# Chunks 10 and 11 of k and q through TensorE transposes, and a reordered load list, in a windowed-attention and SwiGLU kernel

## The chip, the core and the metric

The program runs on one core of one Trainium2 chip. The metric is the time of one execution on the device in microseconds (us): the median over several runs. Beside it there is one execution recorded by the hardware profiler, whose instructions, DMAs and idle times are the views quoted in this document.

## What is computed

Attention over 8 batches of 8 heads, with 576 positions of 64 elements each, where each position sees itself and the 63 before it. Its output, as 4608 tokens of 512 elements, goes through a gated feed-forward block.

```python
scores = scale * np.matmul(q, k.transpose(0, 1, 3, 2))
mask = (rel >= 0) & (rel < window)          # window = 64, rel = query - key
attn = softmax of scores where mask holds
x = np.matmul(attn, v), laid out as (4608, 512)
g = x @ w_gate                              # (512, 1536)
silu = g * (1.0 / (1.0 + np.exp(-g)))
val = x @ w_val                             # (512, 1536)
return (silu * val @ w_out)                 # (1536, 512)
```

q, k, v and the weights lie in HBM as float32; the kernel casts them to bf16 on the way in.

## The kernel before, in words

**Tiles.** The 4608 tokens are 36 chunks of 128. Attention works on a chunk at a time, mostly in pairs; the feed-forward block works on groups of 512 tokens (`c` = 0 to 8), so four chunks feed one group. For each chunk the scores (`S`, `Sb`, `S2`, `Sx`: L459 to L534) need k and q with the head dimension on the partitions (`kT`, `qT`), the product with v (`AV2`, `B2`: L602, L712) needs the probabilities `pt` and the values `va`, and its normalised result `xb` is transposed (`X`: four TensorE transposes at L804, or one DMA transpose at L791) into `xT`, which feeds the group.

**The feed-forward block.** `F(c, fs)` computes `hT` for the 128-row blocks `fs` of the 1536 hidden rows: four matmuls of 128x512 by `Wg`, four by `Wv` (L908), a tanh on ScalarE (L889), two operations on VectorE (L894, L896). `F(c, (a, b), lo, hi)` does two blocks on half of the tokens, with matmuls of 128x256. `O` and `O2` (L950) multiply `hT` by `Wo`, twelve matmuls for each 128 tokens, and store.

**Four ways to kT and qT.** (1) Chunks 0 to 3: loaded in a row layout (`first_loads`, `next_load`), transposed by `first_T`. (2) `load2` brings a pair of chunks into `ks2[st % 2]`, `qs2[st % 2]`, and `T64(st)` does 64 small TensorE transposes (L389: 2 tensors, 8 columns, 2 chunks, 2 halves), evicted in four copies by ScalarE; used for pairs 2 and 4, that is chunks 4, 5 and 8, 9. (3) `next_load(x, 3)` and `T64(3)` do the same for chunks 6 and 7 from the row layout. (4) All others: `load(n, "kq")` on GpSimd's queue and a DMA transpose on SyncE's queue (`T`, L368).

**Buffers that matter here.** Way 1 for chunks 2, 3 and way 3 use one pair of buffers, `ks1` and `qs1`; it is `self.first[x, 1]` (L216, L217), with the keys `("s2", x, 1, 0)` and `("s2", x, 1, 1)`. `load2` for pairs 2 and 4 uses `ks0` and `qs0`.

**What sets the order.** The order is written by hand in `build` (L1040). Each call of `g.op` appends one operation; `_Graph.op` (L43) notes as its dependencies the operations that last wrote what it reads, and those that last read or wrote what it writes, as the program stands at that call. Each engine runs its operations in the order in which they were appended, and waits at each for its dependencies. All loads but the first four DMAs are issued from GpSimd (POOL) in one queue. The program order around the change is this (L1106 to L1115):

```python
        self.Tkq2(2)
        self.late_loads()
        F(0, (7,))
        self.S2(4)
        F(0, (8,))
        F(0, (9,), side=True)
        self.AV2(4)
        F(0, (10,))
        ev = self.T64(3)
```

`early_loads` is called at L1065, while chunks 0 to 3 are worked on, `more_loads` at L1100. PSUM has eight banks, taken in the order of least recent use (`bank`, L230).

Of the kernel before, what the change touches and what calls it, by code (L numbers as in the profile page):

```python
# [152 lines left out]

class _Kernel:
    NQ = 8
    NV = 10
    NZ = 8
    ZQ = 9
# [14 lines left out]
    def alloc(self):  # L173
        nc = self.nc

        def sb(name, n, dtype=BF):
            return nc.alloc_sbuf_tensor(name, [128, n], dtype)

        def ring(name, cnt, n, dtype=BF):
            return [sb("%s%d" % (name, i), n, dtype) for i in range(cnt)]  # L180
# [8 lines left out]
        self.Wo = sb("Wo", NF * DM)[:, :].rearrange("p (c m) -> p c m", c=NF)  # L189
        self.qn = ring("qn", self.NQ, DM)  # L190
        self.kn = ring("kn", self.NQ, DM)
        pair = lambda t: t[:, :].rearrange("p (h j d) -> p h j d", h=H, j=2)
        qs, ks = ring("qs", 2, 2 * DM), ring("ks", 2, 2 * DM)
        self.qs2 = [pair(t) for t in qs]
        self.ks2 = [pair(t) for t in ks]
        self.va = [t[:, :].rearrange("p (h d) -> p h d", h=H) for t in ring("va", self.NV, H * 80)]
        self.vs = [t[:, :].rearrange("p (h d) -> p h d", h=H) for t in ring("vs", 3, H * 80)]
# [41 lines left out]
    def pair(self):  # L239
        if not self.lru:  # L240
            return [self.bank("a"), self.bank("a")]
        ok = [j for j in range(0, 8, 2) if not {j, j + 1} & self.held]
        j = min(ok, key=lambda j: max(self.touched(j), self.touched(j + 1)))
        self.held |= {j, j + 1}
        return [(self.ps[i], ("ps", i)) for i in (j, j + 1)]
# [68 lines left out]
    def load(self, n, what="kqv", gate=None):  # L314
# [3 lines left out]
        for x in what:  # L318
            src = {"k": self.k, "q": self.q, "v": self.v}[x]
            if x == "v":  # L320
                dst, nm, i = self.va[n % self.NV], "va", n % self.NV
            else:
                i = n % self.NQ
                dst = (self.kn if x == "k" else self.qn)[i][:, :].rearrange("p (h d) -> p h d", h=H)
# [35 lines left out]
    def T(self, n, x):  # L360
        if n >= NCH:
            return
        i = n % self.NQ
        if x == "k":
# [6 lines left out]
    def T64(self, st):  # L371
        n = 2 * st
        bx = self.two()
        loads = []
        for x in "kq":
            if st == 3:
                loads.append((x, *self.first[x, 1]))
            else:
                loads.append((x, (self.ks2 if x == "k" else self.qs2)[st % 2], [("s2", x, st % 2, i) for i in range(2)]))

        def pe(e):
            for i, (x, src, _) in enumerate(loads):
                for a in range(8):
                    for u in range(2):
                        r = slice(64 * u, 64 * u + 64)
                        for p in range(2):
                            o = bx[u][0].bitcast(BF)[64 * p:64 * p + 64, 512 * i + 64 * a:512 * i + 64 * a + 64]
                            y = src[r, a, p, :] if st == 3 else src[r, 2 * (a // 2) + p, a % 2, :]
                            z = e.transpose(o, y, self.ident[r, r])  # L389
            return z  # L390

        rd = ["ident"] + [k for _, _, ks in loads for k in ks]
        self.g.op("pe", pe, reads=rd, writes=[b[1] for b in bx])

        def ev(x, u, eng):
            bank, bk = bx[u]
            i = "kq".index(x)
            a = bank.bitcast(BF)[:, 512 * i:512 * i + 512]
            z = (n + u) % (self.NZ if x == "k" else self.ZQ)
            d = (self.kT if x == "k" else self.qT)[:, :, 128 * z:128 * z + 128]  # L400
            if st == 3:
                a, d = a.rearrange("p (j g c) -> p c g j", j=8, c=4), d.rearrange("p c (g j) -> p c g j", j=8)
            else:
                a, d = a.rearrange("p (c j t) -> p c t j", c=4, j=2), d.rearrange("p c (t j) -> p c t j", j=2)
            self.copy(eng, d, a, [bk], [(x + "T", z, 0), (x + "T", z, 1)])
            left.discard((x, u))
            if not any(v == u for _, v in left):
                self.held.discard(bk[1])

        left = {(x, u) for x in "kq" for u in range(2)}  # L410
        return ev
# [135 lines left out]
    def AVk(self, st, phase):  # L547
        n, bx, av, done = st
        iv, jv, ip, jp = n % self.NV, (n - 1) % self.NV, n % self.NP, (n - 1) % self.NP
        lone = [(2 * n) % BPB == 0, (2 * n + 1) % BPB == 0]  # L550
# [35 lines left out]
    def AVmm(self, st, phase):  # L586
        n, bx, av, done = st
        iv, jv, ip = n % self.NV, (n - 1) % self.NV, n % self.NP
        va, vb, pt = self.va[iv], self.va[jv], self.pt[ip]
# [82 lines left out]
    def unit(self, n, h, r, c):  # L672
        iv, jv, ip, jp = n % self.NV, (n - 1) % self.NV, n % self.NP, (n - 1) % self.NP
        rows = slice(64 * r, 64 * r + 64)
        back = r == 1 and c == 0
        va = self.va[jv if back else iv][rows, h, 0:65]
        if n < self.KW:
            return self.pt[ip][rows, h, 64 * c:64 * c + 64], va
        if c != r and (2 * n + c) % BPB == 0:
            return None  # L680
        x0 = 0 if c == r else 64
        return self.pt[jp if back else ip][rows, h, x0:x0 + 64], va

    def AVpair(self, n):
# [6 lines left out]
        def part(m, phase, js, after=None):  # L691
# [22 lines left out]

            iv, jv, ip, jp = m % self.NV, (m - 1) % self.NV, m % self.NP, (m - 1) % self.NP
            rd = [("pt", a, p) for a in ({ip, jp} if m >= self.KW else {ip}) for p in range(2)]
# [65 lines left out]
    def X(self, n, eng="sp", kind="f"):  # L782
        if n >= NCH:
            return
        g = self.g
        ix, it, u = n % 4, (n // 4) % self.NX, n % 4
        xb = self.xb[ix]
        xo = self.xT[it][:, :, 128 * u:128 * u + 128]
        xk = [("xb", ix, 0), ("xb", ix, 1)]
        if eng == "sp":  # L790
            g.op("sp", lambda e: e.dma_start_transpose(xo, xb[:, :]), reads=xk, writes=[("xT", it, u)], dma=True)  # L791
            return
        self.Xp(n, kind)(eng)
# [122 lines left out]
    def F(self, c, fs, lo=0, hi=512, mid=None, side=False):  # L916
        do = self.Fp(c, fs, lo, hi, side)
        for a in range(len(fs)):
            do("Wg", a)
        if mid:  # L920
            mid()
        do("tan", 0)
        for a in range(len(fs)):
            do("Wv", a)
        do("end", 0)
# [4 lines left out]
    def O(self, c, u, mid=None):  # L930
        io = (4 * c + u) % self.NO
        self.Omm(c, u, 0, 512, "act", [("ost", io), ("osth", io)], mid=mid)
        self.store(c, u)
# [70 lines left out]
    def early_loads(self):  # L1004
        self.load2(2, "k")
        self.load2(2, "q")
        self.W(8, 10)
        self.W(10, 12)
        self.load(4, "v")
        self.load(5, "v")  # L1010

    def more_loads(self):
        self.next_load("k", 3)
        self.next_load("q", 3)
        self.load_wo(0, 6)
        self.load_wo(6, 12)
        self.load(6, "v")
        self.load(7, "v")

    def late_loads(self):  # L1020
        for n in (10, 11):
            self.load(n, "kq")
        self.load2(4, "k")
        self.load2(4, "q")
        for n in (8, 9):
            self.load(n, "v")
        for n in (12, 13):
            self.load(n, "kq")

    def loop_loads(self, n):  # L1030
        for m in (n + 6, n + 7):
# [8 lines left out]
    def build(self):  # L1040
        F, S, AV, X, O = self.F, self.S, self.AV, self.X, self.O
# [68 lines left out]
        F(0, (8,))  # L1110
        F(0, (9,), side=True)
        self.AV2(4)
        F(0, (10,))
        ev = self.T64(3)
        ev("k", 0, "act")  # L1115
        ev("q", 0, "act")
        X(4, "act")
        F(0, (11,), mid=lambda: X(5, "act"))
        ev("k", 1, "act")
        ev("q", 1, "act")  # L1120
        F(1, (0, 1), 0, 256)
        self.S2(6)
        F(1, (2, 3), 0, 256)
        O(0, 0)
        self.AV2(6)
        for n in (10, 11):
            self.Tkq(n)

        def mid():
            X(6, "act")  # L1130
            X(7, "dve")

        O(0, 1, mid)
        F(1, (4,))
        self.init_kmask()
        F(1, (5,))
        self.Tkq2(4)
        for n in (10, 11):
            self.load(n, "v", self.lastF)
        for n in (12, 13):  # L1140
            self.Tkq(n)
        F(1, (6,))
        self.S2(8)
        F(1, (7,))
        self.O2(0, 2)
        self.B2(8)
        self.store(0, 2)
        X(8)
        X(9)
        F(1, (0, 1), 256, 512)  # L1150
        F(1, (8,))
        for n in (14, 15):
            self.load(n, "kq", self.lastF)
        F(1, (2, 3), 256, 512)
        self.O2(0, 3)
        self.B2(10)
        self.store(0, 3)
        F(1, (9,))
        self.T(14, "k")
        X(10)  # L1160
        X(11)
# [10 lines left out]
        for c in range(2, NFC):  # L1172
            for u in range(4):
                n = 4 * c + u + 4
# [6 lines left out]
                v = u + 1 if c == 2 else u  # L1181
# [71 lines left out]
```

## Time and profile before

| | us |
|---|---|
| runs | 329.48, 328.05, 329.32 |
| median | 329.32 |
| profiled execution | 327.78 |
| its span, first to last instruction | 325.9 |
| TensorE (PE) busy | 319.0 |
| VectorE (DVE) busy | 215.6 |
| ScalarE (ACT) busy | 125.8 |
| GpSimd (POOL) busy | 104.1 |

The profiled execution lasts 1.88 us longer than its span. PE is matmuls, PEld weight loads that overlap them, SP is SyncE; a q behind an engine's name (POOLq, SPq) marks a DMA that it issued. In a timeline row stand the start, the duration of the merged group, engine, line, operation, output<-inputs, shape and count, and in brackets the idle time of the engine just before and what ended it. In a row of DMA issues the last number is the time from issue to landing, when its semaphore tells that all data is there. L12 is line 12 of the kernel.

### The profile page before, as it was taken

What the parts mean: (1) busy time and instruction counts of PE and PEld (TensorE: products, weight loads), DVE (VectorE), ACT (ScalarE), POOL (GpSimd) and SP (SyncE); (2) the same over time, 40 slices, a digit from 0 to 9 for tenths busy, and PEclk for the clock granted to TensorE, in tenths of its full rate; (3) what the DMA queues carried; (4) which work ended last, traced back from release to release, by engine and by line L of the source; (5) the groups of instructions that cost most, each with busy time, mean ns of one, the idle gap of its engine ahead of it and who ended that gap; (6) DMA issues with size and microseconds to landing.
All of it is one profiled execution on the core that took longest, in us unless ns stands there. A gap on an engine that the chain in (4) does not pass through costs nothing.

```text
span 325.9 us, 7911 instructions
## 1 busy us (share of the span) xinstructions
PE 319.0 (98%) x3374; PEld 161.9 (50%) x3374; DVE 215.6 (66%) x400; ACT 125.8 (39%) x227; POOL 104.1 (32%) x134
## 2 busy tenths in 40 slices
PE   7999999899999999999999999999999999999996
PEld 5654564465444554545444454545454544444444
DVE  6776875588485967675858595858676767555510
ACT  3836554634232533333324242424242421322311
POOL 6999832041726052607060606151402000000000
PEclk9999999999999999999999999999999999999999
DMA  7999999999999979979999997999796404000012
GB/s 187 178 192 186 206 172 174 146 140 149 154 152 155 134 86 148 154 122 145 131 102 126 141 153 74 139 137 131 102 116 92 74 32 66 32 32 34 32 64 97
DMA packets 154354, 39.83 MB, mean 122 GB/s; under 512 B 140368, under 2 KB 149328, under 8 KB 154320
## 3 DMA queue, kind: packets, MB, share of 16 engines
q0 software_dynamic: 104896, 18.36, 72.4%
q1 hardware_dynamic: 43952, 11.15, 23.8%
q10 hardware_dynamic: 5472, 9.83, 9.8%
q8 instruction: 26, 0.43, 0.6%
q14 instruction: 8, 0.07, 0.1%
HBM read 37.75 MB, written 9.44 MB: 145 GB/s over the span
## 4 chain that ended last, share of the span: by engine, by line
PE 94%; DMA 2%; POOL 2%; DVE 1%; issue 1%
PE ps L908 58%; PE ps L950 29%; PE ps L712 2%; DMA Wv<-in_moe_w_val_dram 2%; PE ps L534 2%; PE ps L484 1%; POOL va L330 1%; PE ps L389 1%; PE ps L488 1%; PE ps L602 0%; PE ps L804 0%; POOL ks L828 0%; PE ps L565 0%; POOL qs L828 0%; POOL Wg L345 0%
## 5 line engine op out<-in xcount | busy, mean ns | idle before, releaser
L894 DVE SCALAR_TENSOR_TENSOR uu<-sig,ps 128x512 bf16<-128x512 bf16 x108 | 73.8, 683 | 57.6 <-ACT sig L889 57.2
L908 PE MATMUL ps<-xT,Wv 128*128 128x512 bf16 (+1 forms) x456 | 110.9, 368 | 0.5 <-DMA Wv<-in_moe_w_val_dram 0.5
L908 PE MATMUL ps<-xT,Wg 128*128 128x512 bf16 (+1 forms) x456 | 111.1, 368 | 0.0
L889 ACT ACTIVATE sig<-ps 128x512 bf16<-128x512 f32 x108 | 65.2, 604 | 90.3 <-PE ps L908 90.3
L950 PE MATMUL ps<-Wo,hT 128*128 128x512 bf16 (+1 forms) x444 | 98.8, 373 | 0.0
L896 DVE SCALAR_TENSOR_TENSOR hT<-uu,ps 128x512 bf16<-128x512 bf16 x108 | 74.2, 687 | 4.2 <-PE ps L908 0.5
L908 PEld LDWEIGHTS ps<-xT,Wv 128*128 128x128 bf16 x456 | 44.5, 98 | 49.1 <-DMA Wv<-in_moe_w_val_dram 0.6
L950 PEld LDWEIGHTS ps<-Wo,hT 128*128 128x128 bf16 x444 | 43.3, 98 | 49.2
L908 PEld LDWEIGHTS ps<-xT,Wg 128*128 128x128 bf16 x456 | 42.7, 98 | 45.3 <-ACT xT L260 0.4
L330 POOL DMA_DIRECT2D kn<-in_k_dram x29 | 24.9, 861 | 109.7 <-PE ps L908 105.4
L330 POOL DMA_DIRECT2D va<-in_v_dram x40 | 34.2, 885 | 33.5 <-PE ps L908 33.5
L260 ACT ACTIVATE ost<-ps 128x512 f32<-128x512 f32 (+1 forms) x22 | 12.9, 588 | 52.9 <-PE ps L950 52.9
L261 DVE COPY ost<-ps 128x512 f32<-128x512 f32 (+1 forms) x15 | 10.1, 674 | 30.9 <-PE ps L950 30.9
L544 ACT ACTIVATE pt<-ps 128x512 bf16<-128x512 f32 x36 | 18.6, 602 | 29.0 <-PE ps L534 29.0
L330 POOL DMA_DIRECT2D qn<-in_q_dram x29 | 25.1, 871 | 0.3 <-issue 0.3
L496 ACT ACTIVATE pt<-ps 128x512 bf16<-128x512 f32 x28 | 14.5, 615 | 13.2 <-PE ps L488 13.2
L747 DVE TENSOR_TENSOR xb<-ps,rc 128x512 bf16<-128x512 f32 (+2 forms) x39 | 18.8, 509 | 0.5
L712 PE MATMUL ps<-va,pt 64*64 64x65 bf16 x800 | 12.5, 192 | 0.8 <-issue 0.8
L510 DVE TENSOR_TENSOR pt<-pt,kmask 128x1024 bf16<-128x1024 bf16 x18 | 11.5, 681 | 0.0
L712 PEld LDWEIGHTS ps<-va,pt 64*64 64x64 bf16 x800 | 10.4, 107 | 0.9 <-issue 0.9
L743 DVE RECIPROCAL rc<-ps 128x8 f32<-128x8 f32 (+2 forms) x39 | 5.7, 173 | 7.6 <-PE ps L712 7.1
L510 DVE TENSOR_TENSOR pt<-pt,mask 128x1024 bf16<-128x1024 bf16 x14 | 9.2, 685 | 0.4 <-ACT pt L496 0.3
(76 smaller groups left out, 132.5 us busy)
## 6 DMA issues: line engine op xcount, KB each, us to landing
out_dram<-ost ACTq DMA_DIRECT2D x35, 256.0 KB, 3.1
va<-in_v_dram POOLq DMA_DIRECT2D x32, 128.0 KB, 5.3
kn<-in_k_dram POOLq DMA_DIRECT2D x23, 128.0 KB, 4.5
qn<-in_q_dram POOLq DMA_DIRECT2D x23, 128.0 KB, 4.5
Wg<-in_moe_w_gate_dram POOLq DMA_DIRECT2D x6, 256.0 KB, 6.6
Wv<-in_moe_w_val_dram POOLq DMA_DIRECT2D x6, 256.0 KB, 7.7
Wo<-in_moe_w_out_dram POOLq DMA_DIRECT2D x2, 768.0 KB, 17.0
ks<-in_k_dram POOLq DMA_DIRECT2D x2, 256.0 KB, 7.4
```

The source lines that it names most:

```text
L260: return self.g.op("act", lambda e: e.activation(d, a, ACTF.Copy), reads=reads, writes=writes, after=after)
L330: self.g.op("pool", lambda e, d=d, a=a: e.dma_start(d, a), writes=ks, dma=True, after=gate)
L496: g.op("act", lambda e, po=po, p=p: e.activation(po, sv[p], ACTF.Exp, scale=SCALE), reads=[bx[p][1]], writes=[pk[p]])
L510: self.g.op("dve", lambda e: e.tensor_tensor(pt, pt, m, ALU.mult), reads=pk + mk, writes=pk)
L544: g.op("act", lambda e, po=po, p=p: e.activation(po, sv[p], ACTF.Exp, scale=SCALE), reads=[bx[p][1]], writes=[pk[p]])
L712: x = e.matmul(o, ab[0], ab[1], start=first, stop=phase == 1, skip_group_check=True)
L747: g.op("dve", lambda e, av=av, hs=hs, w=w, rc=rc, xo=xo: e.tensor_tensor(xo[:, :, hs, :], av[:, :, :, 0:64], rc[:, :, hs].unsqueeze(3).to_ ...
L889: g.op("act", lambda e: e.activation(sig[:, 0:w], G[:, 0:w], ACTF.Tanh, scale=0.5), reads=[gk], writes=[("sig", i)])
L894: g.op("dve", lambda e: e.scalar_tensor_tensor(uu[:, 0:w], sig[:, 0:w], 1.0, G[:, 0:w], ALU.add, ALU.mult), reads=[("sig", i), gk], writes ...
L896: g.op("dve", lambda e: e.scalar_tensor_tensor(out, v3(uu), 0.5, v3(V), ALU.mult, ALU.mult), reads=[("uu", i), vk], writes=[("hT", ih, f) ...
L908: r = e.matmul(bank[:, a * n:a * n + n], W[:, kk, f * 128:f * 128 + 128], xT[:, kk, lo:hi], start=(kk == 0), stop=(kk == NK - 1))
L950: r = e.matmul(OB[:, 0:n], hT[:, f, 128 * u:128 * u + 128], self.Wo[:, f, lo:hi], start=(f == 0), stop=(f == NF - 1))
```

## The change

`ROWS = (3, 5)` lets `T64(5)` take chunks 10 and 11 in the row layout, as `T64(3)` does for 6 and 7. Their `load(n, "kq")` and their four DMA transposes go; `next_load("k", 5)` and `next_load("q", 5)` come, in `late_loads`, into the buffers of `self.first[x, 1]`. `next_load` for pair 3 moves into `early_loads`, ahead of `W(10, 12)`, as do the values of chunks 4 and 5. The values of chunks 10 and 11 are loaded at the end of `late_loads` and no longer wait for a matmul group. `T64(3)` moves from behind `F(0, (10,))` to directly behind `AV2(4)`, `Tkq2(4)` from behind `F(1, (5,))` to directly behind `AV2(6)`, and `Tkq2(5)` stands directly behind `S2(8)`. The blocks of group 1 are run in another order: blocks 4 and 5 in two halves, 6 and 7 whole but later, 8 and 9 earlier. The calls of L1106 to L1112 stay as they are.

```diff
--- before.py
+++ after.py
@@ -153,6 +153,7 @@
 
 class _Kernel:
     NQ = 8
+    ROWS = (3, 5)
     NV = 10
     NZ = 8
     ZQ = 9
@@ -373,7 +374,7 @@
         bx = self.two()
         loads = []
         for x in "kq":
-            if st == 3:
+            if st in self.ROWS:
                 loads.append((x, *self.first[x, 1]))
             else:
                 loads.append((x, (self.ks2 if x == "k" else self.qs2)[st % 2], [("s2", x, st % 2, i) for i in range(2)]))
@@ -385,7 +386,7 @@
                         r = slice(64 * u, 64 * u + 64)
                         for p in range(2):
                             o = bx[u][0].bitcast(BF)[64 * p:64 * p + 64, 512 * i + 64 * a:512 * i + 64 * a + 64]
-                            y = src[r, a, p, :] if st == 3 else src[r, 2 * (a // 2) + p, a % 2, :]
+                            y = src[r, a, p, :] if st in self.ROWS else src[r, 2 * (a // 2) + p, a % 2, :]
                             z = e.transpose(o, y, self.ident[r, r])
             return z
 
@@ -398,7 +399,7 @@
             a = bank.bitcast(BF)[:, 512 * i:512 * i + 512]
             z = (n + u) % (self.NZ if x == "k" else self.ZQ)
             d = (self.kT if x == "k" else self.qT)[:, :, 128 * z:128 * z + 128]
-            if st == 3:
+            if st in self.ROWS:
                 a, d = a.rearrange("p (j g c) -> p c g j", j=8, c=4), d.rearrange("p c (g j) -> p c g j", j=8)
             else:
                 a, d = a.rearrange("p (c j t) -> p c t j", c=4, j=2), d.rearrange("p c (t j) -> p c t j", j=2)
@@ -1005,27 +1006,29 @@
         self.load2(2, "k")
         self.load2(2, "q")
         self.W(8, 10)
-        self.W(10, 12)
         self.load(4, "v")
         self.load(5, "v")
-
-    def more_loads(self):
         self.next_load("k", 3)
         self.next_load("q", 3)
+        self.W(10, 12)
+
+    def more_loads(self):
         self.load_wo(0, 6)
         self.load_wo(6, 12)
         self.load(6, "v")
         self.load(7, "v")
 
     def late_loads(self):
-        for n in (10, 11):
-            self.load(n, "kq")
         self.load2(4, "k")
         self.load2(4, "q")
         for n in (8, 9):
             self.load(n, "v")
+        self.next_load("k", 5)
+        self.next_load("q", 5)
         for n in (12, 13):
             self.load(n, "kq")
+        for n in (10, 11):
+            self.load(n, "v")
 
     def loop_loads(self, n):
         for m in (n + 6, n + 7):
@@ -1110,52 +1113,49 @@
         F(0, (8,))
         F(0, (9,), side=True)
         self.AV2(4)
-        F(0, (10,))
         ev = self.T64(3)
         ev("k", 0, "act")
         ev("q", 0, "act")
+        ev("k", 1, "act")
+        ev("q", 1, "act")
+        F(0, (10,))
         X(4, "act")
         F(0, (11,), mid=lambda: X(5, "act"))
-        ev("k", 1, "act")
-        ev("q", 1, "act")
         F(1, (0, 1), 0, 256)
         self.S2(6)
         F(1, (2, 3), 0, 256)
         O(0, 0)
+        F(1, (4, 5), 0, 256)
         self.AV2(6)
-        for n in (10, 11):
-            self.Tkq(n)
+        self.Tkq2(4)
 
         def mid():
             X(6, "act")
             X(7, "dve")
 
         O(0, 1, mid)
-        F(1, (4,))
+        F(1, (8,))
         self.init_kmask()
-        F(1, (5,))
-        self.Tkq2(4)
-        for n in (10, 11):
-            self.load(n, "v", self.lastF)
+        self.S2(8)
+        self.Tkq2(5)
         for n in (12, 13):
             self.Tkq(n)
-        F(1, (6,))
-        self.S2(8)
-        F(1, (7,))
+        F(1, (9,))
+        F(1, (0, 1), 256, 512)
         self.O2(0, 2)
         self.B2(8)
         self.store(0, 2)
         X(8)
         X(9)
-        F(1, (0, 1), 256, 512)
-        F(1, (8,))
+        F(1, (2, 3), 256, 512)
+        F(1, (6,))
         for n in (14, 15):
             self.load(n, "kq", self.lastF)
-        F(1, (2, 3), 256, 512)
+        F(1, (4, 5), 256, 512)
         self.O2(0, 3)
         self.B2(10)
         self.store(0, 3)
-        F(1, (9,))
+        F(1, (7,))
         self.T(14, "k")
         X(10)
         X(11)
```

## The prediction

> **What bounds the kernel now.** I read the page's list of busy time first, then the chain that ended last.
>
> ```profile
> PE 319.0 (98%) x3374; PEld 161.9 (50%) x3374; DVE 215.6 (66%) x400; ACT 125.8 (39%) x227; POOL 104.1 (32%) x134
> PE 94%; DMA 2%; POOL 2%; DVE 1%; issue 1%
> ```
>
> TensorE is busy for 319.0 of 325.9 us, and 94% of the chain is TensorE. So a microsecond in which TensorE stands still, or one more of its work, is a microsecond of the kernel, and nothing else counts unless TensorE waits for it. The timeline of TensorE, searched for bracketed idle time from 16 us on, has only three entries:
>
> ```profile
> 16.64 1.05 PE L908 MATMUL ps<-xT,Wv 128*128 128x256 bf16 x8 [0.46 <-DMA Wv<-in_moe_w_val_dram]
> 58.52 0.22 PE L488 MATMUL ps<-qT,kT 64*64 64x64 bf16 x2 [0.60 <-issue]
> 65.21 0.44 PE L712 MATMUL ps<-va,pt 64*64 64x65 bf16 x26 [0.82 <-issue]
> ```
>
> The last two, 1.42 us, lie in the middle of blocks whose waits stand at their start, and the profile finds no producer for them. That is all that better hidden loads could win here. Next comes the place where the change puts its first transposes, again in TensorE's timeline.
>
> ```profile
> 34.82 0.88 PE L602 MATMUL ps<-va,pt 64*64 64x65 bf16 x64
> 35.63 1.04 PE L908 MATMUL ps<-xT,Wg 128*128 128x512 bf16 x4
> 36.51 1.03 PE L908 MATMUL ps<-xT,Wv 128*128 128x512 bf16 x4
> 37.46 0.45 PE L389 MATMUL ps<-ident,ks 64*64 64x64 bf16 x32
> 37.74 0.43 PE L389 MATMUL ps<-ident,qs 64*64 64x64 bf16 x32
> ```
>
> `AV2(4)` (L602) hands over at 35.63 to `F(0, (10,))`; `T64(3)` (L389) starts at 37.46, without idle time: its rows have long landed. After the change `T64(3)` is due at 35.6.
>
> **The change, part by part.** *The wait that it adds.* In program order `late_loads` (L1107) stands ahead of `AV2(4)` and `T64(3)` (L1112, L1114), and stays there. The change puts `next_load("k", 5)` and `next_load("q", 5)` into it, and these write `self.first[x, 1]`: `ks1`, `qs1`, the one pair of buffers that `T64(3)` reads. A dependency is noted against the last writer in program order, so `T64(3)` now waits for the loads of pair 5, not for those of pair 3. (It then transposes the rows of chunks 10 and 11 in place of those of 6 and 7, and `T64(5)` the same rows once more; the amount of work is as planned.) TensorE runs in order, so all matmuls stand behind this wait. Its price is the landing of `next_load("q", 5)` less 35.6.
>
> That landing is worked out from the queue of loads. POOL issues faster than the DMAs deliver, and the loads land in the order of issue. The first fence has issue times, from POOL's timeline; the second the narrow windows of the view of DMA issues, one window for each load, in the order of issue (last number: us from issue to landing).
>
> ```profile
> 24.91 0.71 POOL L828 DMA_DIRECT2D ks<-in_k_dram  x1
> 25.61 0.71 POOL L828 DMA_DIRECT2D qs<-in_q_dram  x1
> 26.32 1.67 POOL L350 DMA_DIRECT2D Wo<-in_moe_w_out_dram  x2
> 27.96 1.77 POOL L330 DMA_DIRECT2D va<-in_v_dram  x2
> 29.70 0.91 POOL L330 DMA_DIRECT2D kn<-in_k_dram  x1
> 33.16 1.44 POOL L339 DMA_DIRECT2D ks<-in_k_dram  x2
> 34.51 0.77 POOL L339 DMA_DIRECT2D qs<-in_q_dram  x1
> 35.85 1.87 POOL L330 DMA_DIRECT2D va<-in_v_dram  x2
> ```
>
> ```profile
> ks<-in_k_dram POOLq DMA_DIRECT2D x1, 256.0 KB, 10.3
> qs<-in_q_dram POOLq DMA_DIRECT2D x1, 256.0 KB, 10.9
> ...
> Wo<-in_moe_w_out_dram POOLq DMA_DIRECT2D x1, 768.0 KB, 17.0
> va<-in_v_dram POOLq DMA_DIRECT2D x1, 128.0 KB, 17.0
> ...
> kn<-in_k_dram POOLq DMA_DIRECT2D x1, 128.0 KB, 17.0
> ...
> ks<-in_k_dram POOLq DMA_DIRECT2D x1, 128.0 KB, 16.8
> ...
> qs<-in_q_dram POOLq DMA_DIRECT2D x1, 128.0 KB, 17.0
> ...
> va<-in_v_dram POOLq DMA_DIRECT2D x1, 128.0 KB, 20.6
> va<-in_v_dram POOLq DMA_DIRECT2D x1, 128.0 KB, 24.8
> ```
>
> The rows of pair 3 landed at 24.91 + 10.3 = 35.2 (k) and 25.61 + 10.9 = 36.5 (q): 1.3 us for 256 KB. The second `Wo` was issued half way through its row, near 27.2, and landed at 44.2. The first value chunk behind it landed at 27.96 + 17.0 = 45.0, and two loads of 128 KB later k of chunk 10 at 46.7: 0.85 us each. The first part of `load2(4)` landed at 33.16 + 16.8 = 50.0, and two parts later the first of q at 34.51 + 17.0 = 51.5: 0.75 us each.
>
> Up to the second `Wo` the change issues the same loads in another order, so 44.2 holds. Behind it now come `v` 6 and 7 (2 x 0.85 = 1.7), four parts of `load2(4)` (3.0), `v` 8 and 9 (1.7), and pair 5 (2 x 1.3 = 2.6). 44.2 + 9.0 = 53.2. POOL is no limit: it is done with `v` 6 and 7 at 29.7, and six issues of 0.7 to 0.9 us later, near 34, it issues pair 5, far ahead of the delivery. **The stall is 53.2 - 35.6 = 17.6 us.** Its bounds: at least 16.6 (each of the ten loads behind `Wo` 0.1 us quicker), at most 26, if pair 5 met what `v` 9 met in the trace (35.85 and half of 1.87, plus 24.8: 61.6). I take 17.6, since what slowed `v` 8 and 9 were the first DMA transposes and output stores on other queues, and neither is there while TensorE stands still:
>
> ```profile
> 46.75 1.29 SPq L368 DMA_TRANSPOSE kT<-kn  x1
> 48.06 0.36 ACTq L968 DMA_DIRECT2D out_dram<-ost  x1
> ```
>
> The first is one of the four transposes that the change removes; the second comes behind `O(0, 0)`, which stands behind the wait. Nobody else covers the stall: `F(0, (10,))`, which could have run at 35.63, is queued behind it on TensorE, and ACT and DVE live from TensorE's output.
>
> *The clock after the stall.* No idle time of over 0.82 us stands in the trace after the first matmuls, so what 17 us of idleness do to TensorE is shown only by its start, where it comes from idleness as well:
>
> ```profile
> 1.40 4.10 PE L867 MATMUL ps<-wz 128*128 128x224 f32 x10 [1.40 <-DVE wz L264]
> 5.34 1.03 PE L847 MATMUL ps<-ident,ost 128*128 128x128 bf16 x8
> 6.62 0.73 PE L847 MATMUL ps<-ident,ost 128*128 128x128 bf16 x8 [0.25 <-DVE ost L261]
> ...
> 50.08 0.61 PE L804 MATMUL ps<-ident,xb 128*128 128x128 bf16 x8
> ```
>
> ```profile
> L804 PE MATMUL ps<-ident,xb 128*128 128x128 bf16 x32 | 3.0, 220 | 0.3 <-DVE xb L646 0.2
> L847 PE MATMUL ps<-ident,ost 128*128 128x128 bf16 x16 | 1.8, 279 | 0.2 <-DVE ost L261 0.2
> ```
>
> Eight transposes of 128x128 take 1.03 us at 5.34, 0.73 at 6.62, and 0.61 later. Without the last one's own duration (the means of the second fence: 0.28 and 0.22 us) seven steps take 0.75 against 0.39: half speed, from 1.40 until near 6.8, some way into the group of 6.62. Half of these 5.4 us is lost: 2.7 us. Bounds: nothing, if idleness in mid-program doesn't slow TensorE, and 2.9, half of 5.8, if the whole group of 6.62 belongs to the slow stretch. I take 2.7, the nearest row's. The Trainium skill ("TensorE: Matmul & The Clock Gate", Part 1) says that the array's clock is halved after an idle window of about 3.4 us and returns after one busy window of that length, whose phase is free; by it the slow stretch would be 3.4 to 6.8 us and the loss, an estimate from that page, 1.7 to 3.4. The stretch of 5.4 us at the start lies within that.
>
> *The transposes added and moved.* From the chain in order of time:
>
> ```profile
> 54.86 0.64 PE ps L389 x64
> 55.50 1.83 PE ps L908 x8
> ...
> 97.90 5.18 PE ps L908 x24
> ```
>
> `T64(5)` is another 64 transposes: +0.64 us. Eight matmuls in a long run take 5.18 / 3 = 1.73, directly behind a block of small ones 1.83: 0.10 for the change of kind. `T64(3)` and `Tkq2(4)` now share that with `AV2(4)` and `AV2(6)`: -0.2; `T64(5)` shares it with `S2(8)`. Its four evictions are ACT's, at 0.6 us (row L260, below), between others, and ACT is busy for 39% only; their first reader is `Sx(10)`, three matmul blocks later. If that cover were gone, it would be some 2 us once.
>
> ```profile
> L260 ACT ACTIVATE kT<-ps 128x512 bf16<-128x512 bf16 x6 | 3.6, 606 | 2.8 <-PE ps L389 2.8
> ```
>
> *The loads and the rest.* `W(10, 12)` now lands after pair 3, at 36.5, where the queue stood before after the same bytes; `F(0, (10,))` first needs it after the stall. `v` 10 and 11 come without a gate; TensorE never waited for them. Blocks of group 1 in another order are the same matmuls; two halves instead of two wholes cost under 0.1. These parts: 0. The two idle entries of 1.42 us fall 19 us later, when the backlog of loads is through. The matmul blocks with the same kinds of steps in the later rows of the timeline have no idle time, so I take -1.4; bounds 0 (they come back in the denser bursts) and +0.8 (one more).
>
> **Sum:** 17.6 + 2.7 + 0.64 - 0.2 - 1.4 = +19.3 us. On the profiled execution's 327.78 (span 325.9 and 1.88 around it) that is 347.1; on the median of the runs shown, 329.32, it is 348.6. Since medians will be compared, I forecast **348.6 us**.
>
> **The rivals.** *Late landing* (chance 0.05): pair 5 meets other queues as `v` 9 did, stall 26, 329.32 + 26 + 2.7 - 1.0 = 357.0. For it: the rows 20.6 and 24.8. Against it: neither SP nor ACT has anything to issue until TensorE goes on, but for SP's transposes of chunks 12 and 13, whose rows are behind pair 5.
>
> *Early landing* (0.05): pair 5 doesn't queue behind all of `load2(4)`, `v` 8 and 9 (4.7 us) and TensorE's clock is spared the slow stretch: 348.6 - 4.7 - 2.7 = 341.2. Against it: the landing times above rise in the order of issue.
>
> *The other side: no stall* (0.04). The place is `T64(3)`'s dependency, and the price is the whole 17.6 + 2.7. The point from which it decides: whether the rows that it waits for have landed by 35.6. Those of pair 3, now ahead of two weight loads of 256 KB (1.3 us each, as its own), land near 36.5 - 2.6 = 33.9; if `T64(3)` waited for them, there would be no stall, and the sum would be +0.64 - 0.2 - 1.4: 328.4. For it speaks this margin of 1.7 us; against it, that L216 and L217 give one buffer for pairs 1, 3 and 5, and that `late_loads` is called ahead of `T64(3)`. It is also the case in which the change does what it says for chunks 6 and 7.
>
> **How the numbers follow.** Forecast 0.86, late 0.05, early 0.05, no stall 0.04. The forecast's own ends: stall 16.6 to 18.6, clock 1.3 (half of the stretch) to 2.9, idle entries -1.4 to +0.8, the runs' own scatter of 328.05 to 329.48: from 328.05 + 16.6 + 1.3 + 0.44 - 1.4 = 345.0 to 329.48 + 18.6 + 2.9 + 0.44 + 0.8 = 352.2. I give 344.5 to 353, and leave the rivals out, whose sum is 0.14. A difference of 0.5% (1.6 us) is about what a measurement of this kernel can tell from none. Slower by more: 0.96; within: 0.025; faster by more: 0.015, both from the last rival.
>
> **What would show it.** In TensorE's timeline one idle entry of some 17 us, ended by the DMA of `ks` or `qs`, ahead of the first L389 group behind L602 at 34.8; pair 5 landing near 53; behind the gap matmuls of L908 at about twice their spacing for 3 to 7 us; four blocks of L389 against three; the two "issue" entries gone; SP without four of its transposes. I am wrong if `T64(3)` starts without a gap, or if the gap ends well before 50.

## The result, and the profile after

| | before | after |
|---|---|---|
| median of 6 runs, us | 328.69 (327.15 to 329.51) | 345.38 (344.62 to 345.99) |
| ratio | | 1.0515, 95% interval 1.048 to 1.055 |
| profiled execution, us | 327.78 | 345.87 |
| its span, us | 325.9 | 344.1 |

The change costs 16.7 us by the medians and 18.1 by the two profiled executions; 348.6 was forecast, in a range of 344.5 to 353. From the page of the changed kernel: busy time, TensorE's busy share and granted clock in forty slices of 8.6 us, and the chain that ended last.

```profile
PE 317.7 (92%) x3417; PEld 165.2 (48%) x3454; DVE 215.8 (63%) x400; ACT 128.0 (37%) x231; POOL 101.9 (30%) x132
PE   8999107999999999999999999999999999999996
PEclk9999755999999999999999999999999999999999
PE 82%; POOL 8%; DMA 7%; issue 2%; DVE 1%; ACT 0%; ACTq 0%; POOLq 0%
```

TensorE's busy time is about what it was (317.7 against 319.0; it reads a little low, as this profile has 3417 matmuls to 3454 weight loads, so some records are missing); the span has grown around it. There is one hole, in the fifth to seventh slices, and the granted clock falls there and stays down when the work is back. POOL and DMA have 8% and 7% of the chain instead of 2% each, since it now leads through a load. The timeline of TensorE at that place:

```profile
34.45 0.88 PE L603 MATMUL ps<-va,pt 64*64 64x65 bf16 x64
53.04 0.64 PE L390 MATMUL ps<-ident,ks 64*64 64x64 bf16 x32 [17.72 <-DMA qs<-in_q_dram]
53.46 0.65 PE L390 MATMUL ps<-ident,qs 64*64 64x64 bf16 x32
54.44 1.49 PE L909 MATMUL ps<-xT,Wg 128*128 128x512 bf16 x3 [0.33 <-issue]
55.72 1.91 PE L909 MATMUL ps<-xT,Wv 128*128 128x512 bf16 x4
```

`AV2(4)` (now L603) starts at 34.45, `T64(3)` (L390) at 53.04, released by the DMA that fills `qs`. (Lines are one higher than before; x3 stands for a group of four of which one record is missing.) POOL's timeline has the issue of that load, and the view of DMA issues its time to landing:

```profile
33.99 0.70 POOL L829 DMA_DIRECT2D ks<-in_k_dram  x1
34.69 0.71 POOL L829 DMA_DIRECT2D qs<-in_q_dram  x1
```

```profile
qs<-in_q_dram POOLq DMA_DIRECT2D x1, 256.0 KB, 18.3
```

34.69 + 18.3 = 53.0, with 53.2 forecast. L829 is `next_load`, and an issue at 34.69 can only be that of pair 5, as pair 3 is issued in `early_loads` (here at 23.30 and 24.00). The windows view shows what the hole does to the clock (columns: start and end, length; then busy time of PE, PEld, DVE, ACT, POOL with the count of instructions; granted clock, DMA share, GB/s):

```profile
36.00:38.20 2.20, 0.00 (x0) 0.00 (x0) 1.88 (x5) 0.00 (x0) 2.20 (x4) 1.00 1.25 208
38.20:53.00 14.80, 0.00 (x0) 0.00 (x0) 0.00 (x0) 0.00 (x0) 3.46 (x5) 0.50 1.72 184
53.00:58.60 5.60, 5.23 (x77) 2.89 (x79) 1.38 (x2) 3.06 (x6) 0.00 (x0) 0.50 2.15 144
58.60:60.00 1.40, 1.40 (x10) 0.71 (x9) 0.00 (x0) 0.54 (x2) 0.00 (x0) 0.97 0.25 49
```

The clock falls to 0.50 some 3 us into the hole, and stays there for 5.6 us after TensorE has work again: 5.6 x 0.5 = 2.8 us lost at most, if TensorE works all the time. The seven recorded matmuls of 128x512 take 3.2 us here, from 54.44 to 57.63; in the kernel before the same group, all eight, takes 1.9, from 35.63 to 37.54.

### The profile page after: what moved, and what is told of

Same layout as the page of the kernel before. It is cut to its first block, busy times and chain, and to the rows that moved or that the text cites. A ratio compares the mean times of both kernels' runs of the same rounds, so it can differ in the third digit from the quotient of the medians.

```text
span 344.1 us, 8023 instructions
## 1 busy us (share of the span) xinstructions
PE 317.7 (92%) x3417; PEld 165.2 (48%) x3454; DVE 215.8 (63%) x400; ACT 128.0 (37%) x231; POOL 101.9 (30%) x132
## 4 chain that ended last, share of the span: by engine, by line
PE 82%; POOL 8%; DMA 7%; issue 2%; DVE 1%; ACT 0%; ACTq 0%; POOLq 0%
PE ps L909 49%; PE ps L951 27%; DMA qs<-in_q_dram 5%; PE ps L713 2%; POOL va L331 2%; PE ps L535 2%; DMA hT<-in_q_dram 1%; POOL Wg L346 1%; POOL Wv L346 1%; POOL qs L340 1%; POOL vs L262 1%; POOL ks L340 1%; PE ps L485 1%; POOL Wo L351 0%; DVE hT L897 0%
## 5 line engine op out<-in xcount | busy, mean ns | idle before, releaser
L909 PE MATMUL ps<-xT,Wg 128*128 128x512 bf16 (+1 forms) x445 | 108.0, 367 | 3.1 <-issue 2.7
L909 PEld LDWEIGHTS ps<-xT,Wv 128*128 128x128 bf16 x464 | 45.5, 98 | 48.3 <-issue 1.1
L909 PEld LDWEIGHTS ps<-xT,Wg 128*128 128x128 bf16 x464 | 43.9, 98 | 46.0 <-issue 1.1
L331 POOL DMA_DIRECT2D kn<-in_k_dram x27 | 23.0, 854 | 133.5 <-PE ps L909 133.5
L331 POOL DMA_DIRECT2D qn<-in_q_dram x27 | 23.2, 862 | 5.1 <-DMA Wo<-in_moe_w_out_dram 5.1
L390 PE MATMUL ps<-ident,ks 64*64 64x64 bf16 x128 | 2.0, 206 | 17.7 <-DMA qs<-in_q_dram 17.7
L261 ACT ACTIVATE kT<-ps 128x512 bf16<-128x512 bf16 x8 | 4.9, 612 | 22.4 <-PE ps L390 22.4
L390 PEld LDWEIGHTS ps<-ident,ks 64*64 64x64 bf16 x128 | 1.7, 118 | 18.3 <-issue 17.8
```

The costliest lines, as they stand in the source:

```text
L261: return self.g.op("act", lambda e: e.activation(d, a, ACTF.Copy), reads=reads, writes=writes, after=after)
L331: self.g.op("pool", lambda e, d=d, a=a: e.dma_start(d, a), writes=ks, dma=True, after=gate)
L909: r = e.matmul(bank[:, a * n:a * n + n], W[:, kk, f * 128:f * 128 + 128], xT[:, kk, lo:hi], start=(kk == 0), stop=(kk == NK - 1))
```

## The experiments

The theory: `T64(3)` waits because pair 5 is loaded, in program order ahead of it, into the buffers that it reads; the length of the wait is the landing of pair 5; the clock adds 2.8 us. The rivals: the new order of the loads brings pair 3 or the weights too late for the moved transposes; and the slow matmuls behind the wait are no matter of the clock. In all experiments the ratio is to the kernel before on the same chip.

### e1_own_buffers: pair 5 in buffers of its own

```diff
-        qs, ks = ring("qs", 2, 2 * DM), ring("ks", 2, 2 * DM)
+        qs, ks = ring("qs", 3, 2 * DM), ring("ks", 3, 2 * DM)
...
+            self.first[x, 5] = d5, [("s2", x, 2, 0), ("s2", x, 2, 1)]
...
-                loads.append((x, *self.first[x, 1]))
+                loads.append((x, *self.first[x, 5 if st == 5 else 1]))
...
-        d, keys = self.first[x, 1]
+        d, keys = self.first[x, 5 if st == 5 else 1]
```

> The changed kernel with a third pair of buffers, used by pair 5 alone; the order of all loads and steps stays. Theory (T64(3) waits because pair 5 is loaded into the buffers that it reads): T64(3) starts directly behind AV2(4), near 35.6 us, no idle time of over 1 us in TensorE, no half clock; 345.4 - 17.7 - 2.8 = 325 if all else stays as in the changed kernel, 328.4 if the backlog of loads keeps costing what it cost before. Rival 1 (the new order of loads brings pair 3 or the weights too late for the moved T64(3)): the gap stays, 343 to 346 us.

Measured: 326.67 us (326.24 to 327.99), ratio 0.9951 (0.9929 to 0.9973). TensorE's timeline:

```profile
35.08 0.88 PE L605 MATMUL ps<-va,pt 64*64 64x65 bf16 x64
35.81 0.45 PE L392 MATMUL ps<-ident,ks 64*64 64x64 bf16 x32
36.07 0.45 PE L392 MATMUL ps<-ident,qs 64*64 64x64 bf16 x32
```

The order of every load and step is that of the changed kernel, and `T64(3)` follows `AV2(4)` without a gap. The rival on the order of the loads falls: the whole loss hangs on the shared buffer. 18.7 us come back (345.38 against 326.67), less than the 20.5 worked out from gap and clock; the point on the clock, below, takes this up.

### e2_pair5_behind: the loads of pair 5 appended behind T64(3)

```diff
     def late_loads(self):
...
+    def later_loads(self):
         self.next_load("k", 5)
         self.next_load("q", 5)
...
         ev = self.T64(3)
+        self.later_loads()
```

The loads that follow pair 5 in the list (`k` and `q` of 12 and 13, the values of 10 and 11) move along.

> The changed kernel with the loads of pair 5 and all loads behind them appended behind T64(3) instead of ahead of it; the buffers stay shared. Theory: T64(3) waits for pair 3 again and has no gap; pair 5 waits on POOL until T64(3) has read, near 36.3 us, and lands near 53, ahead of T64(5) at some 57; 325 to 329 us. Rival 1 (order of pair 3 and of the weights): gap stays, 343 to 346. Rival 2 (the wait only moves to T64(5)): a gap ahead of T64(5), 330 us or more.

Measured: 326.20 us (326.10 to 327.17), ratio 0.9938 (0.9913 to 0.9963). TensorE's timeline, then POOL's, then the landing of `qs` of pair 5:

```profile
34.76 0.88 PE L603 MATMUL ps<-va,pt 64*64 64x65 bf16 x64
35.49 0.45 PE L390 MATMUL ps<-ident,ks 64*64 64x64 bf16 x32
...
55.88 0.44 PE L390 MATMUL ps<-ident,ks 64*64 64x64 bf16 x32
```

```profile
36.52 0.70 POOL L829 DMA_DIRECT2D ks<-in_k_dram  x1 [2.44 <-PE ps L390]
37.21 0.71 POOL L829 DMA_DIRECT2D qs<-in_q_dram  x1
```

```profile
qs<-in_q_dram POOLq DMA_DIRECT2D x1, 256.0 KB, 16.7
```

With the same two buffers the dependency turns round: POOL waits 2.44 us until `T64(3)` has read, which costs nothing, as the queue of DMAs behind it is full. Pair 5 lands at 37.21 + 16.7 = 53.9, and `T64(5)` starts at 55.88, so the wait doesn't move there. This version beats the changed kernel and, by about 2 us, the one before; e1_own_buffers stands beside it within their scatter. By the order of the calls, both also give `T64(3)` the rows of its own pair back, which the changed kernel doesn't.

### e3_pair5_sooner: pair 5 ahead of load2(4) and the values of 8 and 9

```diff
     def late_loads(self):
+        self.next_load("k", 5)
+        self.next_load("q", 5)
         self.load2(4, "k")
         self.load2(4, "q")
         for n in (8, 9):
             self.load(n, "v")
-        self.next_load("k", 5)
-        self.next_load("q", 5)
```

> The changed kernel with pair 5 loaded ahead of load2(4) and the values of chunks 8 and 9, so directly behind those of 6 and 7. Theory: the gap is the landing of pair 5, which now comes at 46.4 + 2.6 = 49.0 instead of 52.95, so the gap is some 4.0 us shorter, 13.7, and the time 345.4 - 4.0 = 341.4, within the 1 us that the phase of the clock may add or take. Rival 1: the gap and the time stay at 345.4, as nothing ahead of Wo is moved.

Measured: 341.23 us (340.89 to 341.76), ratio 1.0398 (1.0364 to 1.0431), with 341.4 expected. In TensorE's timeline the gap is 13.76 us instead of 17.72; POOL's timeline has the issue of the load that ends it:

```profile
48.86 0.64 PE L390 MATMUL ps<-ident,ks 64*64 64x64 bf16 x32 [13.76 <-DMA qs<-in_q_dram]
```

```profile
34.65 0.71 POOL L829 DMA_DIRECT2D qs<-in_q_dram  x1 [1.21 <-DMA qs<-in_q_dram]
```

The loads taken out from ahead of pair 5, 4.7 us by the prediction's rates, were worth 4.0 us of gap and 4.15 of time. The load was issued no sooner than in the changed kernel (34.65 against 34.69), since it waited for pair 3 to land in the same buffer, and still landed 4 us sooner. So the length of the wait is the place in the queue, not the time of issue.

### e4_filler and e5_filler_80: work within the wait

```diff
+        self.fill(70)
         ev = self.T64(3)
...
+    def fill(self, count):
+        bank, bk = self.bank("a")
+        def pe(e):
+            for _ in range(count):
+                r = e.matmul(bank[:, :], self.ident[:, :], self.wz[:, :], start=True, stop=True)
+            return r
+        self.g.op("pe", pe, reads=["wz", "ident"], writes=[bk])
```

e5_filler_80 has `self.fill(80)` in its place.

> The changed kernel with 70 matmuls of 128x512 (zeros times the identity, into a free PSUM bank, read by nobody) between AV2(4) and T64(3): 15.1 us of work within the wait of 17.7. Theory on the clock (idleness halves it, and 2.8 us are lost after the wait): clock 1.0 throughout, matmuls of L909 behind the wait 216 ns apart, 345.4 - 2.8 = 342.6 us. Rival (the slow matmuls behind the wait come from the load on the DMAs or from the operands): unchanged, 345.4 us.

Measured: 345.54 us (343.57 to 345.76), ratio 1.0511 (1.046 to 1.0562): a miss, and its time alone is the number of the rival. The gap that the filler left, and the windows behind it:

```profile
53.15 0.45 PE L390 MATMUL ps<-ident,ks 64*64 64x64 bf16 x32 [2.75 <-DMA qs<-in_q_dram]
```

```profile
50.90:54.30 3.40, 0.92 (x65) 0.85 (x67) 0.00 (x0) 0.38 (x1) 0.00 (x0) 1.00 2.07 167
54.30:57.70 3.40, 3.40 (x13) 1.44 (x11) 1.16 (x2) 2.36 (x6) 0.00 (x0) 0.50 2.54 156
57.70:60.00 2.30, 2.30 (x18) 1.33 (x17) 0.32 (x2) 1.50 (x3) 0.00 (x0) 1.00 0.49 73
```

2.75 us of idleness were enough: in the first window TensorE was busy for 0.92 of 3.4 us. The transposes of `T64(3)` still ran at full speed, and then the clock was 0.50 for 3.4 us, 1.7 us lost. Of the four runs, of which one has a profile (345.40), three had a mean clock of 0.995 and took 345.4 to 345.8; the fourth had 1.000 and took 343.57. So the filler had to be longer:

> The changed kernel with 80 filler matmuls (zeros times the identity, read by nobody) instead of the 70 of e4_filler, whose 15.1 us left 2.75 us of idle time, behind which the clock still fell to a half for 3.4 us. 80 x 0.216 = 17.3 us leave some 0.4 us. Theory on the clock (idleness within a window of some 3.4 us halves it): 1.0 throughout, 345.4 - 2.8 = 342.6 us. Rival (the load on the DMAs or the operands slow the matmuls behind the wait): half spacing stays, 344 to 345.5 us.

Measured: 343.82 us (343.69 to 343.95), ratio 1.047 (1.0405 to 1.0535), mean clock 1.000 in all four runs.

```profile
53.49 0.45 PE L390 MATMUL ps<-ident,ks 64*64 64x64 bf16 x32 [1.05 <-DMA qs<-in_q_dram]
...
55.03 1.03 PE L919 MATMUL ps<-xT,Wv 128*128 128x512 bf16 x4
```

Four matmuls by `Wv` take 1.03 us instead of 1.91, at a DMA share as high as in the changed kernel (2.29 from 53.4 to 58.0, against 2.15), and on the same operands. The theory on the clock holds, and its rival falls. By the medians 1.6 us came back, not the 2.8 expected; by the two profiled executions 2.0. Of the difference 0.45 us is a later landing (the transposes start at 53.49 instead of 53.04); from there to the end of `B2(10)` the profile shows 2.5 us less.

### e6_no_pair5, e7_before_again, e8_no_transposes: the idle entries without a releaser

e1 and e2 are faster than the kernel before, although TensorE has 64 transposes more. The prediction expects such a gain from the two entries near 58 and 65 us. These three runs start from the kernel before; in e6 and e8 the scores of chunks 10 and 11 are formed from older contents of `kT` and `qT`.

```diff
 e6_no_pair5, in late_loads:
-        for n in (10, 11):
-            self.load(n, "kq")
 e6_no_pair5 and e8_no_transposes, in build:
-        for n in (10, 11):
-            self.Tkq(n)
```

> The kernel before without the loads of k and q of chunks 10 and 11 and without their four DMA transposes; the scores of these chunks are formed from what lies in kT and qT from earlier chunks, all other work and order stay. Theory (the two idle entries of 0.60 and 0.82 us without a releaser come from the load on the DMAs between 55 and 66 us): both gone, 328.6 - 1.4 = 327.2 us or a little less. Rival (they belong to places in TensorE's instructions, or to how the small blocks stand): both stay near 58 and 65 us, 328.6 us.

> The kernel before, unchanged, for a second profile. Theory: the two idle entries without a releaser come back near 58 and 65 us, as they belong to this stage's load on the DMAs; time within 327.1 to 330.1 us. Rival: they are chance, and are elsewhere or missing.

Measured: e7, unchanged, 329.16 us; e6 326.79 us (325.48 to 327.50), ratio 0.9936 (0.9909 to 0.9963). The idle entries of more than 0.2 us from 40 us on, first of e7, then of e6:

```profile
42.48 0.24 PE L484 MATMUL ps<-qT,kT 64*64 64x128 bf16 x2 [0.35 <-issue]
51.28 0.51 PE L804 MATMUL ps<-ident,xb 128*128 128x128 bf16 x6 [0.90 <-issue]
59.98 0.22 PE L488 MATMUL ps<-qT,kT 64*64 64x64 bf16 x2 [0.95 <-issue]
66.81 0.44 PE L712 MATMUL ps<-va,pt 64*64 64x65 bf16 x26 [0.97 <-issue]
```

```profile
43.12 0.24 PE L484 MATMUL ps<-qT,kT 64*64 64x128 bf16 x2 [0.40 <-issue]
51.33 0.51 PE L804 MATMUL ps<-ident,xb 128*128 128x128 bf16 x6 [0.35 <-issue]
```

The second profile of the kernel before has four entries, 3.17 us in all, against 1.42 in two in the first; the last two stand at the same instructions as there. So they belong to this stage, but their number and length differ from run to run. Without pair 5 those two are gone, while TensorE's program is the same, instruction by instruction: TensorE's own sequence alone doesn't make them. Which part of pair 5 brings them?

> The kernel before with the loads of k and q of chunks 10 and 11 kept, but without their four DMA transposes; the scores of these chunks are formed from what lies in kT and qT from earlier chunks, all other work and order stay. Of what e6_no_pair5 took away, which part brings the idle entries near 58 and 65 us? If the transposes (they sit beside the loads from 47 to 61 us): both gone, 326.8 us as in e6_no_pair5. If the bytes of the loads: both stay, 328.6 us. If both count: between.

Measured: 327.05 us (325.40 to 327.38), ratio 0.9938 (0.9913 to 0.9963): as e6. Its only entry of more than 0.2 us from 40 us on is

```profile
44.53 0.81 PE L950 MATMUL ps<-Wo,hT 128*128 128x512 bf16 x3 [0.29 <-issue]
```

The loads stay, the four DMA transposes go, and so do the entries at 58 and 65 us. The values of chunk 9 show how much longer a load takes beside these transposes: issued by POOL near 36.7, they needed 24.8 us to land in the kernel before, and here

```profile
va<-in_v_dram POOLq DMA_DIRECT2D x1, 128.0 KB, 18.3
```

So of the some 2 us by which e1 and e2 beat the kernel before, about 1.5 (328.52 against 327.05) come with four DMA transposes fewer beside a full queue of loads; the rest is not shown. What exactly TensorE waits for in such an entry is not shown: the profile names no releaser, and no run here takes it apart. The traces hold one hint. All eight such entries of the two profiles of the kernel before and of e6 end 2.2 to 2.4 us after the start of a 16 KB packet of the queue that the profile calls "instruction" (in the kernel before one starts between 62.9 and 63.1, and the entry ends at 65.21); the short one of e8 doesn't. That TensorE waits there for its next instructions is a rival that no run here tests.

## Why the prediction was right, point by point

- **The wait that it adds**: right in cause and size. 17.6 us forecast, 17.72 measured; landing at 53.2 forecast, 53.0 measured. e1 and e2 show the shared buffer as the cause, e3 the place in the queue as the length. *Late landing* did not happen: SyncE's first DMA transpose of this stretch is issued at 53.95, after the wait. *Early landing* did not either.
- **No stall**, the rival on the other side, is what e1 and e2 are. Its condition was right (the rows of pair 3 are there in time: `T64(3)` has no gap); of its price, 1.0 us less than the kernel before, e1 shows 1.9 and e2 2.4. The term that is too small is the next one.
- **The idle entries**: the mis-sized term of the sum. -1.4 was read from one profile with 1.42 us of them; a second profile has 3.17. With the 0.44 forecast for the transposes taken as it stands, e1 and e2 put this term at -2.4 and -2.8 instead, an estimate from their medians. e8 ties 1.5 us of it to the DMA transposes; that the rest is idle entries too is argued, not shown. This and the clock are most of the step from 19.3 us forecast to 16.7 measured; by the two profiled executions the difference is 18.1. The forecast time is a further 0.6 us high because it stands on 329.32, the median of three runs, where six give 328.69.
- **The clock after the stall**: right in kind, forecast at 2.7 us; 5.6 x 0.5 = 2.8 read from the changed kernel's windows, 2.5 in the stage by e5, and in the time 1.6, or some 2.0 with e5's later landing of 0.45 added. The changed kernel's runs have a mean clock of 0.970 (345.66 to 345.99) or of 0.975 (344.62 to 345.11). 0.005 of 344 us is 1.7 us, or 3.4 us at half clock: an estimate, but as long as the stretch in e4. The profile is one of the first kind, so the median holds less of this loss than the profile. The 5.6 us measured lie within the estimate of 3.4 to 6.8 us that the prediction works out from the Trainium skill's page "TensorE: Matmul & The Clock Gate" (Part 1). Where that page asks for no idle gaps of more than some 3 us between bursts ("Why this matters for your kernels"), the profile of e4 shows 2.75 us to be too much already. What the prediction took from the kernel's start, half speed until near 6.8, the granted clock doesn't confirm: the windows view of the kernel before reads 1.00 there, although the matmuls stand twice as far apart as later.

```profile
1.40:6.90 5.50, 5.25 (x22) 4.29 (x23) 4.10 (x20) 2.48 (x4) 3.90 (x7) 1.00 0.86 234
```

So a 1.00 in that view proves little by itself, and the reading of e5 rests on its matmuls of 1.03 us.

- **The transposes added and moved**: 0.64 - 0.2 forecast. In e2, `S2(8)` with `T64(5)` behind it takes 1.5 us, from 55.18 to near 56.7; `S2(8)` took 1.6 before, with an idle entry of 0.6 in it. So the added block cost about 0.5. No run measures the moves alone; at 0.2 us the runs' scatter would hide them.
- **The loads and the rest** at nothing: right. No wait of over 0.2 us for a weight or a value appears in TensorE's timeline after the change.

## What to carry to other kernels

Where dependencies are noted in program order, a prefetch written ahead of the last reader of its buffer doesn't wait for that reader: the reader waits for the prefetch, and reads its data. Before moving a load, list for its buffer the writers and readers in the order in which the code appends them; here that list alone shows the wait, and either a further buffer or the same loads appended behind the reader take it away. In a queue that is full, the length of the wait is found by adding up what stands ahead of the load.

## What the runs showed of the hardware that was not expected

A gap of 2.75 us in TensorE's work was followed by 3.4 us at half clock, and these began 1.15 us after the work had come back (53.15 and 54.30), so that the slow matmuls don't stand next to the gap that caused them. Behind an idle time of 1.05 us (e5) the matmuls ran at full spacing. A load's time of issue did not set its landing while the queue was full: in e3 a load issued at 34.65 landed 4 us sooner than one issued at 34.69 in the changed kernel. And without four DMA transposes on SyncE's queue, beside a full queue of loads, the kernel was about 1.5 us faster by the medians (328.52 against 327.05 in e8), though in the profile none of the idle entries that went with them is a wait for one.
